# Eight filler matmuls on TensorE while VectorE finishes the last head

## The chip, the cores and the metric

One core of a Trainium2 chip. The metric is the device time of one launch in microseconds (us); lower is better. The runs of the kernel before agree within 0.2%. The profile is of one such execution, and its span, from the first to the last instruction, is some 1.9 us shorter than the device time. Every kernel here was run in the same rounds as the kernel before, on the same chip (three chips in all).

## The reference, cut to what matters

One decode step of grouped-query attention over a cache of 65,536 positions (4 key/value heads, 32 query heads of 128), mixed by a gate with a small gated MLP:

```python
def _A_ref(x, k_cache, v_cache, wq, wo):
    q = (x @ wq) ...                       # 1 x 1024 @ 1024 x 4096
    scores = einsum('bhqd,bhkd->bhqk', q, k) * Dh ** (-0.5)
    p = softmax(scores)
    o = einsum('bhqk,bhkd->bhqd', p, v)
    return o.reshape(1, 1, 4096) @ wo      # 4096 x 1024
...
return g * a + (1 - g) * b                 # g: a sigmoid gate, b: the MLP
```

There is one query row, so every weight and every cache entry is used once. The whole work is to read 162 MB and touch each number once.

## The kernel before

The end of the kernel. Per key/value head it computes scores (`k_tile`), a softmax (`stats`), and the weighted sum over V (`v_tile`). `head_out` turns one head's sum into a column block of `oa`, mostly on VectorE. `project` then multiplies `oa` by A_wo.

```python
WO_SPLIT = ((16,), (8, 4, 2, 1, 1))
...
def head_out(g):
    # DVE: mask the PSUM sum (L447), reduce it (L451)
    # PE:  L455 om_ps <- ls,hsel   (needs the softmax sums only)
    #      L457 om_ps <- o_sb,hsel (needs DVE's L451)
    # DVE: five short ops; the last (L469) writes oa
...
# the end:
for j, n, at in ((0, 2, 1), (2, 1, 3), (3, 1, 4)):
    for i, vt in enumerate(load_kv(A_v_cache, G - 1, j, at, n)):
        v_tile(G - 1, j + i, vt)
head_out(G - 1)

wo_view = A_wo.rearrange("(p c) n -> p c n", c=OC)
c0 = 0
for at, split in enumerate(WO_SPLIT):
    for n in split:
        t = load(wo_view[:, c0:c0 + n, :], (n, D), ...)
        project(t, n, oa, c0, last=(c0 + n == OC))   # 4*n matmuls of 32 columns x 256
        c0 += n
nc.scalar.copy(out=out_sb[:], in_=out_ps[:])         # then two small stores
```

The loads (`load`) are all issued by SyncE on one queue, as soon as their part of the buffer `kv` is free. PE runs its matmuls in program order.

## Time and profile before

| | before |
|---|---|
| device time, median of the first 3 runs | 383.24 us |
| span of the profile | 381.4 us |
| PE busy, DVE busy | 232.4 us (61%), 218.4 us (57%) |
| read from HBM | 162.01 MB, 425 GB/s over the span |
| mean granted TensorE clock | 0.82 |

The page of the profile cuts the span into 40 slices. A digit is the busy share in tenths (9 is 90% or more); the row PEclk is the granted TensorE clock in tenths.

```profile
PE   0433467678157944796397629872967196849355
...
PEclk9966659998759895989588959895799679969766
DMA  9999999999999999999999999999999999999995
```

The DMA engines are busy from the first slice to the last but one. No other engine is. PE (TensorE) is at nine tenths or more in 7 of the 40 slices only, and its clock keeps dropping.

The chain of waits that ended last, its end in order of time (start, length, what):

```profile
346.96 0.04 issue
347.00 31.88 DMA kv<-in_A_wo_dram
378.88 0.04 issue
378.92 0.43 PE out_ps L478 x3
379.35 0.02 issue
379.37 0.37 ACT out_sb L521
```

The chain is a load from 347.00 to 378.88. The last projection matmuls, a copy and the store follow. Only 0.43 us of this is work whose speed depends on the TensorE clock.

The timeline of PE at the end (start, length, line, what, how often; in brackets PE's idle time before it and what ended that):

```profile
359.20 5.92 PE L437 MATMUL o_ps<-kv,pt 128*64 128x512 bf16 x32 [6.08 <-DMA kv<-in_A_v_cache_dram]
365.05 0.23 PE L455 MATMUL om_ps<-ls,hsel 128*32 128x4 f32 x2
368.34 0.64 PE L457 MATMUL om_ps<-o_sb,hsel 128*32 128x128 f32 x2 [3.07 <-DVE o_sb L451]
370.37 4.62 PE L478 MATMUL out_ps<-kv,oa 128*32 128x256 bf16 x96 [1.39 <-DVE oa L469]
376.33 0.62 PE L478 MATMUL out_ps<-kv,oa 128*32 128x256 bf16 x16 [1.34 <-DMA kv<-in_A_wo_dram]
377.60 1.08 PE L478 MATMUL out_ps<-kv,oa 128*32 128x256 bf16 x12 [0.64 <-DMA kv<-in_A_wo_dram]
378.92 0.41 PE L478 MATMUL out_ps<-kv,oa 128*32 128x256 bf16 x4 [0.24 <-DMA kv<-in_A_wo_dram]
```

PE idles for 3.07 and 1.39 us while DVE works on the last head; these are the gaps that the change fills. The projection's first 96 matmuls take 4.62 us. After them PE waits for a load three more times.

In this profile the granted clock changes only at instants of a grid of 3.41 us. Busy time in stretches between such instants (stretch; its length, then PE, PEld (weight loads), DVE (VectorE), ACT, POOL busy, granted clock, DMA share, GB/s):

```profile
363.84:367.26 3.42, 1.44 (x14) 0.41 (x6) 2.07 (x2) 0.00 (x0) 0.00 (x0) 1.00 1.04 446
367.26:370.67 3.41, 0.93 (x10) 0.43 (x14) 2.23 (x6) 0.00 (x0) 0.00 (x0) 0.50 0.91 389
370.67:374.08 3.41, 3.41 (x72) 2.54 (x68) 0.00 (x0) 0.00 (x0) 0.00 (x0) 0.50 0.96 401
374.08:377.50 3.42, 1.53 (x48) 1.14 (x41) 0.00 (x0) 0.00 (x0) 0.00 (x0) 1.00 0.88 343
377.50:380.91 3.41, 1.42 (x16) 0.50 (x15) 0.00 (x0) 0.37 (x1) 0.00 (x0) 0.50 0.11 38
```

The clock is at half (0.50) in most of the projection, and again at the very end.

### The profile page before, as it was taken

Reading aid. Unit: us, or ns where it says so; the run is one execution under the profiler, and the core shown is the slowest. Engines: PE = TensorE matmul, PEld = TensorE weight load, DVE = VectorE, ACT = ScalarE, POOL = GpSimd, SP = SyncE. Lnnn points to the kernel's source line nnn. Section 1 sums busy time; section 2 is a strip of 40 time slices with the busy share of each in tenths; the row PEclk is TensorE's granted clock in tenths of the full one; section 3 lists DMA queues with packets and bytes.
Section 4 is the critical chain, followed back from the end, with each engine's and each line's share of the span. In section 5 each row is a group of like instructions: output and inputs, shape, how many; then the busy total and the mean of one; then the engine's idle time right before and its main releaser. Section 6 shows DMA issues by size and latency. Waiting matters only on the chain.

```text
span 381.4 us, 2581 instructions
## 1 busy us (share of the span) xinstructions
PE 232.4 (61%) x1372; PEld 56.8 (15%) x796; DVE 218.4 (57%) x211; ACT 39.6 (10%) x55; POOL 4.4 (1%) x10
## 2 busy tenths in 40 slices
PE   0433467678157944796397629872967196849355
PEld 0110011112011210121011101120111011212123
DVE  4241487996687506966977059669780488550040
ACT  1010001111601100114010001050001010500000
POOL 4000000000000000000000000000000000000000
PEclk9966659998759895989588959895799679969766
DMA  9999999999999999999999999999999999999995
GB/s 376 439 426 416 433 436 440 436 461 429 400 426 440 440 435 426 440 440 440 440 428 440 440 440 433 428 427 406 433 440 428 426 433 427 440 411 436 440 405 230
DMA packets 4375, 162.17 MB, mean 425 GB/s; under 512 B 520, under 2 KB 524, under 8 KB 908
## 3 DMA queue, kind: packets, MB, share of 16 engines
q1 hardware_dynamic: 4324, 162.01, 98.7%
q8 instruction: 8, 0.13, 0.1%
q14 instruction: 3, 0.02, 0.0%
q10 hardware_dynamic: 40, 0.01, 0.0%
HBM read 162.01 MB, written 0.00 MB: 425 GB/s over the span
## 4 chain that ended last, share of the span: by engine, by line
DMA 59%; PE 20%; DVE 16%; issue 2%; ACT 1%; SPq 1%; DVEq 0%; ACTq 0%
DMA kv<-in_A_k_cache_dram 37%; PE s_ps L391 15%; DVE kv L384 9%; DMA kv<-in_A_wo_dram 8%; DMA kv<-in_A_wq_dram 7%; DMA kv<-in_A_v_cache_dram 7%; PE o_ps L437 3%; DVE pt L427 2%; DVE mx L386 1%; DVE o_sb L451 1%; PE q_ps L277 1%; ACT sc L424 1%; DVE rowt L447 1%; ACT sc L402 1%; SPq L167 1%
## 5 line engine op out<-in xcount | busy, mean ns | idle before, releaser
L391 PE MATMUL s_ps<-kv,wt 128*128 128x512 bf16 x512 | 142.1, 437 | 81.8 <-DVE kv L384 81.7
L384 DVE STREAM_TRANSPOSE kv<-kv 128x2048 int32<-128x2048 int32 x64 | 142.7, 2280 | 55.5 <-DMA kv<-in_A_k_cache_dram 55.5
L437 PE MATMUL o_ps<-kv,pt 128*64 128x512 bf16 x512 | 61.6, 399 | 7.7 <-DMA kv<-in_A_v_cache_dram 7.7
L391 PEld LDWEIGHTS <-wt 128*128 128x128 bf16 x256 | 27.5, 108 | 197.6 <-issue 140.2
L402 ACT CAST sc<-s_ps 128x1024 bf16<-128x1024 f32 x16 | 16.2, 1013 | 253.5 <-PE s_ps L391 253.5
L437 PEld LDWEIGHTS <-pt 128*64 128x64 bf16 x256 | 16.0, 115 | 50.7 <-issue 48.1
L427 DVE STREAM_TRANSPOSE pt<-sc 128x1024 bf16<-128x1024 bf16 x16 | 18.6, 1217 | 6.8 <-ACT sc L424 6.8
L386 DVE TENSOR_REDUCE mx<-sc 128x1 f32<-128x1024 bf16 x12 | 14.5, 1207 | 10.1 <-ACT sc L402 10.1
L424 ACT ACTIVATE sc<-sc,nb 128x1024 bf16<-128x1024 bf16 x16 | 18.2, 1137 | 12.2 <-DVE nb L420 12.2
L447 DVE TENSOR_TENSOR rowt<-o_ps,own 128x1024 f32<-128x1024 f32 x4 | 4.8, 1194 | 24.9 <-PE o_ps L437 24.9
L457 PE MATMUL om_ps<-o_sb,hsel 128*32 128x128 f32 x8 | 2.5, 421 | 19.7 <-DVE o_sb L451 19.7
L406 DVE TENSOR_REDUCE mx<-sc 128x1 f32<-128x1024 bf16 x4 | 4.9, 1220 | 14.2 <-ACT sc L402 14.2
L277 PE MATMUL q_ps<-kv,xT 128*32 128x512 bf16 x64 | 7.2, 627 | 7.4 <-DMA kv<-in_A_wq_dram 7.4
L478 PE MATMUL out_ps<-kv,oa 128*32 128x256 bf16 x128 | 6.7, 366 | 3.7 <-DMA kv<-in_A_wo_dram 2.2
L277 PE MATMUL z_ps<-kv,xT 128*32 128x448 bf16 x64 | 6.2, 570 | 3.8 <-DMA kv<-in_B_w_in_dram 3.8
L344 DVE TENSOR_TENSOR rowt<-q_ps,own_b 128x512 f32<-128x512 f32 x2 | 1.3, 686 | 12.5 <-PE q_ps L277 12.5
L451 DVE TENSOR_REDUCE o_sb<-rowt 128x128 f32<-128x1024 f32 x4 | 7.5, 1872 | 0.1
L292 DVE TENSOR_TENSOR rowt<-z_ps,own_b 128x448 f32<-128x448 f32 x2 | 1.2, 620 | 8.5 <-PE z_ps L277 8.5
L233 PE MATMUL xb_ps<-xg,spread 8*128 8x256 bf16 x1 | 0.4, 367 | 9.1 <-DMA xg<-in_gate_w_dram 9.1
L277 PEld LDWEIGHTS <-xT 128*32 128x32 bf16 x64 | 3.0, 139 | 19.4 <-issue 19.3
L478 PEld LDWEIGHTS <-oa 128*32 128x32 bf16 x128 | 4.4, 124 | 6.1 <-issue 3.3
L521 ACT CAST out_sb<-out_ps 128x256 bf16<-128x256 f32 x1 | 0.4, 372 | 45.4 <-PE out_ps L478 45.4
(88 smaller groups left out, 54.8 us busy)
## 6 DMA issues: line engine op xcount, KB each, us to landing
kv<-in_A_k_cache_dram SPq DMA_DIRECT2D x4, 4096.0 KB, 26.8
kv<-in_A_wq_dram SPq DMA_DIRECT2D x2, 4096.0 KB, 32.8
kv<-in_A_v_cache_dram SPq DMA_DIRECT2D x2, 4096.0 KB
kv<-in_B_w_in_dram SPq DMA_DIRECT2D x2, 3584.0 KB, 15.0
kv<-in_A_wo_dram SPq DMA_DIRECT2D x1, 4096.0 KB
kv<-in_B_w_out_dram SPq DMA_DIRECT2D x1, 3584.0 KB
kv<-in_A_wo_dram SPq DMA_DIRECT2D x1, 2048.0 KB, 28.6
kv<-in_A_wo_dram SPq DMA_DIRECT2D x1, 1024.0 KB, 30.7
```

Source lines behind the costliest of these rows:

```text
L277: ins = nc.tensor.matmul(ps[t * B:(t + 1) * B, k * HN:k * HN + n], lhsT=xT[:, i * KH + c:i * KH + c + 1].to_broadcast([P, B]), rhs=w[:, c, ...
L384: nc.vector.transpose(out=kb[:, v * n:(v + 1) * n], in_=kb[:, v * n:(v + 1) * n])
L386: nc.vector.reduce_max(**late.pop())
L391: ins = nc.tensor.matmul(s_ps[:, k * HN:(k + 1) * HN], lhsT=wt[g % 2][:, v, b].rearrange("p a v h -> p (a v h)"), rhs=kx[:, b // 2, b % 2, ...
L402: nc.scalar.copy(out=sct[g, j][:], in_=s_ps[:])
L406: nc.vector.reduce_max(**late.pop())
L424: nc.scalar.activation(out=sct[g, j][:], in_=sct[g, j][:], func=ACT.Exp, scale=SCALE, bias=nb[:, 0:1], accum_out=lss[g][:, j:j + 1])
L427: nc.vector.transpose(out=ptt[g, j][:].rearrange("p c x -> p (c x)"), in_=sct[g, j][:])
L437: ins = nc.tensor.matmul(o_ps[g][hs, e, :], lhsT=ptt[g, j][:, 2 * u:2 * u + 2, :].rearrange("p c x -> p (c x)"), rhs=vx[:, 2 * u + e], sta ...
L447: nc.vector.tensor_tensor(out=om8, in0=o_ps[g][:].rearrange("p e (v d) -> p (e v) d", d=DH), in1=own_8[:].unsqueeze(2).to_broadcast([P, 2 ...
L451: nc.vector.tensor_reduce(out=o_sb[:], in_=om8.rearrange("p x d -> p d x"), axis=AX.X, op=ALU.add)
L478: nc.tensor.matmul(out_ps[t * B:(t + 1) * B, :], lhsT=vec[:, c0 + c:c0 + c + 1].to_broadcast([P, B]), rhs=w[:, c, t * NO:(t + 1) * NO], st ...
```

## The change

The intent: while VectorE finishes the last head, PE is idle, its clock is halved, and the projection runs at half speed. Eight matmuls into a spare PSUM bank, in two groups, are to keep PE busy enough that the clock stays full. Their operands are the masked weights of an earlier head (mostly zeros), and nobody reads their result.

```diff
+    def keep_busy(n):
+        ps = pss.tile([P, 2 * HN], FP32, name="busy_ps", tag="s")
+        w = wt[G % 2][:].rearrange("p v b t u h -> p (v b t u h)")
+        for i in range(n):
+            ins = nc.tensor.matmul(ps[:, :HN], lhsT=w[:, :P], rhs=w[:, :HN], start=True,
+                                   stop=True, skip_group_check=True)
+            if i > 0:
+                same_weights(ins)
...
             v_tile(G - 1, j + i, vt)
+    keep_busy(4)
     head_out(G - 1)
+    keep_busy(4)
```

In PE's program order the first group stands after the last `v_tile` and before L455; the second after L457 and before the projection. Nothing moves on the other engines. The added lines shift the later line numbers: L478 becomes L487, L521 becomes L532.

## The prediction

> **What bounds the kernel now.** Moving bytes. The profile's page shows the DMA engines at nine tenths or more in 39 of 40 slices, 162.01 MB at 425 GB/s; PE is busy 61%. The chain of waits ends in loads: A_v_cache lands at 339.7, the five A_wo loads are issued from 345.20 to 347.0, and the last one lands at 378.88. After that only this remains: the last PE matmuls of L478 (0.43 us in the chain), the ACT copy (0.37), and the store until 381.4.
>
> **What the clock does.** The windows view shows the granted clock changing between 0.50 and 1.00 only, and only on a grid of 3.413 us: up at 343.36, down at 357.02, up at 363.84, down at 367.26, up at 374.08, down at 377.50. The Trainium skill, "TensorE: Matmul & The Clock Gate", Part 1, gives a free-running window of 3413 ns: agreed. But here the clock falls without a fully idle window. PE was busy 1.44 us of 363.84-367.26, and 1.53 us of 374.08-377.50, and the clock fell; with 2.56 us of a window it stayed. Elsewhere 1.45 to 1.62 us sometimes sufficed: the boundary is near 1.5 us.
>
> **What the change adds.** Nothing is removed. Two PE groups, each one weight load and four 128x512 matmuls: one after the last v_tile, before the om_ps matmuls; one after them, before the projection. Their bank has long been free. By the trace's L437 matmuls (pairs 0.85 us apart at half clock, 0.43 at full), four cost 1.7 us cold, 0.86 warm.
> - Group 1 starts at about 365.1 with the clock full, ends about 366.0. DVE needs until 368.29 for L447 and L451, and L457 waits for that: no delay.
> - Group 2 starts about 369.0, ends at 369.8 (warm) to 370.7 (cold). The projection waits for oa, at 370.31: 0 to 0.4 us delay.
>
> **What it gains.** Group 1 lifts the window 363.84-367.26 to about 2.3 us, so the clock should no longer fall at 367.26. The next window gets L457, group 2 and the projection's start, about 1.5 us: a coin toss whether it falls at 370.67. If it stays full, the first 96 projection matmuls, 4.62 us at half clock, take an estimated 2.6 us (the 16 matmuls at 376.33, at full clock, took 0.62 with the latency of one).
>
> **How much is on the critical path.** Almost none. The 96 matmuls end at 374.99, and PE then waits 1.34 us for the next A_wo load anyway; finishing 2 us earlier only lengthens that wait. The loads were issued 18 us before the change's first instruction, so their landing doesn't move. Only the last four matmuls could gain, at most 0.2 us, if the clock were full at 378.9. But window 374.08-377.50 would hold less PE work than before, so it falls at 377.50 still.
>
> **Time.** 383.2 us, range 382.7 to 383.8; faster by over 2%: 0.01, within 2%: 0.98, slower by over 2%: 0.01.
>
> **What the profile would show.** Eight matmuls near 365 and 369; granted clock 1.00 over 367.3-370.6; the 96 matmuls shorter or the same; PE idle before 376.3 grown from 1.3 to as much as 3.3 us, ended by A_wo; last landing at 378.9 +-0.3; last four matmuls still about 0.4 us; nothing changed before 365.
>
> **What would make it wrong.** The window grid lies elsewhere in the timed runs, the last chunks at full clock (0.2 us less); a group delayed past 371.6 by an unseen semaphore; extra instruction fetches disturbing the loads; a chip with another DMA rate.

## The result

| | before | after |
|---|---|---|
| device time, median (range) of 6 runs | 383.23 us (383.12 to 383.49) | 383.29 us (383.11 to 383.39) |
| span of the profile | 381.4 us | 381.5 us |
| PE busy with the projection's matmuls on A_wo (128 of them) | 6.7 us | 5.0 us |

The ratio is 1.000 with a 95% interval of 0.9987 to 1.0013. (A ratio is the mean time of one kernel's fast runs over that of the other's in the same rounds, so it is not quite the ratio of the medians.)

The chain of waits after the change, its end:

```profile
347.20 31.77 DMA kv<-in_A_wo_dram
378.97 0.04 issue
379.01 0.43 PE out_ps L487 x4
379.44 0.02 issue
379.46 0.37 ACT out_sb L532
```

It is the same chain: the load lands at 378.97 (before: 378.88), then 0.43 us of matmuls.

The timeline of PE after the change:

```profile
365.25 1.04 PE L476 MATMUL busy_ps<-wt 128*128 128x512 bf16 x3
366.21 0.23 PE L455 MATMUL om_ps<-ls,hsel 128*32 128x4 f32 x2
368.54 0.41 PE L457 MATMUL om_ps<-o_sb,hsel 128*32 128x128 f32 x2 [2.10 <-DVE o_sb L451]
368.88 1.04 PE L476 MATMUL busy_ps<-wt 128*128 128x512 bf16 x4
370.34 1.93 PE L487 MATMUL out_ps<-kv,oa 128*32 128x256 bf16 x64 [0.43 <-DVE oa L469]
373.92 1.06 PE L487 MATMUL out_ps<-kv,oa 128*32 128x256 bf16 x32 [1.65 <-DMA kv<-in_A_wo_dram]
376.42 0.62 PE L487 MATMUL out_ps<-kv,oa 128*32 128x256 bf16 x16 [1.44 <-DMA kv<-in_A_wo_dram]
377.69 1.08 PE L487 MATMUL out_ps<-kv,oa 128*32 128x256 bf16 x12 [0.64 <-DMA kv<-in_A_wo_dram]
379.01 0.40 PE L487 MATMUL out_ps<-kv,oa 128*32 128x256 bf16 x4 [0.24 <-DMA kv<-in_A_wo_dram]
```

(One of the first group's four records is missing from the trace.) The groups do what they were made for. The first 96 matmuls of the projection take 1.93 + 1.06 = 2.99 us instead of 4.62. But the row that was one is now two: after 64 matmuls PE waits 1.65 us for the next chunk of A_wo, which lands at about 373.9. Before, the first 64 matmuls at half clock were done at about that time (68 had started by 373.90), so no wait showed. The 1.6 us saved is now waiting, and the chunk after that starts at 376.42, as before (376.33).

The same stretches after the change, on this execution's grid:

```profile
364.15:367.57 3.42, 2.23 (x16) 0.39 (x6) 2.19 (x2) 0.00 (x0) 0.00 (x0) 1.00 0.97 417
367.57:370.98 3.41, 2.02 (x30) 0.86 (x31) 2.11 (x6) 0.00 (x0) 0.00 (x0) 1.00 0.97 413
370.98:374.39 3.41, 1.76 (x68) 1.54 (x64) 0.00 (x0) 0.00 (x0) 0.00 (x0) 1.00 0.97 400
374.39:377.80 3.41, 1.33 (x45) 0.93 (x37) 0.00 (x0) 0.00 (x0) 0.00 (x0) 1.00 0.83 324
377.80:381.21 3.41, 1.25 (x16) 0.34 (x9) 0.00 (x0) 0.37 (x1) 0.00 (x0) 0.50 0.07 26
```

The clock stays full over two boundaries where it was halved before, and then falls at 377.80, because the stretch before that held only 1.33 us of PE work. The last matmuls, the only ones on the chain, run at half clock exactly as before.

### The profile page after: what moved, and what is told of

Same layout as the page of the kernel before. It is cut to its first block, busy times and chain, and to the rows that moved or that the text cites. A ratio compares the mean times of both kernels' runs of the same rounds, so it can differ in the third digit from the quotient of the medians.

```text
span 381.5 us, 2590 instructions
## 1 busy us (share of the span) xinstructions
PE 232.8 (61%) x1379; PEld 56.1 (15%) x798; DVE 218.5 (57%) x211; ACT 39.6 (10%) x55; POOL 4.4 (1%) x10
## 4 chain that ended last, share of the span: by engine, by line
DMA 58%; PE 25%; DVE 13%; ACT 2%; issue 1%; SPq 0%; DVEq 0%; ACTq 0%
DMA kv<-in_A_k_cache_dram 41%; PE s_ps L391 21%; DMA kv<-in_A_wo_dram 8%; DVE kv L384 7%; DMA kv<-in_A_v_cache_dram 7%; PE o_ps L437 3%; DVE pt L427 2%; DMA xg<-in_A_x_dram 2%; DVE o_sb L451 1%; DVE mx L386 1%; ACT sc L402 1%; ACT sc L424 1%; DVE rowt L447 1%; SPq L167 0%; PE om_ps L457 0%
## 5 line engine op out<-in xcount | busy, mean ns | idle before, releaser
L437 PE MATMUL o_ps<-kv,pt 128*64 128x512 bf16 x512 | 61.8, 400 | 7.5 <-DMA kv<-in_A_v_cache_dram 7.5
L437 PEld LDWEIGHTS <-pt 128*64 128x64 bf16 x256 | 16.1, 115 | 50.6 <-issue 48.1
L457 PE MATMUL om_ps<-o_sb,hsel 128*32 128x128 f32 x8 | 2.3, 386 | 18.7 <-DVE o_sb L451 18.7
L487 PE MATMUL out_ps<-kv,oa 128*32 128x256 bf16 x128 | 5.0, 286 | 4.5 <-DMA kv<-in_A_wo_dram 4.0
L532 ACT CAST out_sb<-out_ps 128x256 bf16<-128x256 f32 x1 | 0.4, 372 | 45.2 <-PE out_ps L487 45.2
L487 PEld LDWEIGHTS <-oa 128*32 128x32 bf16 x128 | 3.4, 97 | 6.7 <-issue 5.3
```

Of the source, the lines that this page charges most:

```text
L437: ins = nc.tensor.matmul(o_ps[g][hs, e, :], lhsT=ptt[g, j][:, 2 * u:2 * u + 2, :].rearrange("p c x -> p (c x)"), rhs=vx[:, 2 * u + e], sta ...
L487: nc.tensor.matmul(out_ps[t * B:(t + 1) * B, :], lhsT=vec[:, c0 + c:c0 + c + 1].to_broadcast([P, B]), rhs=w[:, c, t * NO:(t + 1) * NO], st ...
```

## The experiments

Three theories:

- **A.** The landing of the last A_wo load sets the end; PE's speed before it is slack, and the clock can only matter for the last chunk's matmuls.
- **B.** The gain is real but was lost because the clock fell at 377.80, before the last chunks.
- **C.** The groups cost what the clock gains.

Nine kernels were run, one of them (e2) twice. All results were correct except where a wrong one was intended.

### e1: the clock full to the very end

```diff
             project(t, n, oa, c0, last=(c0 + n == OC))
+            keep_busy({16: 4, 8: 4, 4: 2}.get(n, 0))
```

> The changed kernel plus groups of 4, 4 and 2 more busy matmuls after the projections of the first three A_wo chunks, so that the clock stays full until the last matmul. Theory A (the landing of the last A_wo load sets the end): the clock reads 1.00 to the end, the last chunk's four matmuls take about 0.27 us instead of 0.40, the last landing stays at 378.9 +-0.2, time 383.1, at most 0.2 us below the kernel before. Theory B (the gain was lost because the clock fell at 377.80, before the last chunks): 1 us or more faster, 382.2 or less. Theory C (the groups cost what the clock gains): slower than the changed kernel, by up to the 2.2 us that ten more matmuls take at full clock.

Measured: median 383.23 us (383.01 to 383.34), ratio 1.0001 (0.9988 to 1.0014). The last two rows of its PE timeline, where the granted clock reads 1.00:

```profile
378.12 0.29 PE L487 MATMUL out_ps<-kv,oa 128*32 128x256 bf16 x4 [0.27 <-DMA kv<-in_A_wo_dram]
378.77 0.29 PE L487 MATMUL out_ps<-kv,oa 128*32 128x256 bf16 x4 [0.36 <-DMA kv<-in_A_wo_dram]
```

The last four matmuls take 0.29 us instead of 0.40 to 0.41. So the whole possible gain of a full clock at the end is 0.12 us, 0.03% of the time, which the runs can't resolve. Theory B falls. Theory C's loss isn't there either.

### e2 and e3: no A_wo loads, without and with the groups

Both leave out all the loads of A_wo, six in number: the first half in one piece, issued at 333 us in the kernel before, and the five of the second half, which alone the prediction and the expectations count. They project whatever lies in the buffer. The result is wrong (relative error 0.03). e2 is the kernel before with this edit, e3 the changed kernel with it.

```diff
-        t = load(wo_view[:, c0:c0 + n, :], (n, D), at + ...)
+        o0 = int((at + ...) * CT * P)
+        t = kv[:, o0:o0 + n * D].rearrange("p (a b) -> p a b", b=D)
```

> The kernel before with the five A_wo loads left out; the projection reads whatever lies in the buffer, so the result is wrong on purpose. Theory A: the last DMA wait is then A_v_cache's at 359.2, oa comes at 370.3 as before, the 128 projection matmuls run without a stop, at half clock until about 374.1 and then full, some 5.2 us, so the time falls by 3 to 4.5 us, to about 379 to 380. If the loads did not set the end, the time would fall by less than 1 us.

> The changed kernel (both groups) with the five A_wo loads left out; wrong result on purpose. Theory A: without the loads the projection is on the chain, at full clock, about 3.6 us for 128 matmuls, so this kernel is 1.3 to 2 us faster than the same kernel without the groups (the run sent with it). Theory C: no faster than that, since what the clock gains is eaten by the groups themselves.

> The same kernel as e2_noload_plain again, because the profiled execution of that run fell in a state in which every matmul took about twice as long as at half clock (span 794 us) and shows nothing of the tail. Theory A: a fast profile shows the 128 projection matmuls start at about 370.4 without a stop after oa, in 4.5 to 5.5 us against 3.68 in e3_noload_groups, with the clock at half for most of them; time 378.3 to 381.2 as in the fast runs of the first try.

| | fast runs | median | ratio to the kernel before (95%) |
|---|---|---|---|
| e2, without groups | 5 | 380.00 us (378.31 to 381.17) | 0.9908 (0.9889 to 0.9927) |
| e3, with groups, same rounds as e2 | 4 | 377.97 us (377.73 to 378.37) | 0.9864 (0.9851 to 0.9876) |
| e2b, e2 again, later | 4 | 378.64 us (378.39 to 379.71) | 0.9883 (0.9868 to 0.9898) |

The profiled execution of e2 is left out: it fell in a slow state (796.12 us) that is told in the last section. The projection in e2b, then in e3, from their timelines of PE:

```profile
370.30 5.46 PE L487 MATMUL out_ps<-kv,oa 128*32 128x256 bf16 x128 [1.39 <-DVE oa L469]
```

```profile
370.66 3.68 PE L487 MATMUL out_ps<-kv,oa 128*32 128x256 bf16 x128 [0.43 <-DVE oa L469]
```

With the loads gone, the projection runs without a stop and stands on the chain. Now the groups make the projection 1.78 us shorter in the traces (5.46 - 3.68; it ends only 1.43 us earlier, at 374.37 against 375.80, since `oa` came 0.36 us later in e3's execution), and the runs of the same rounds differ by 1.7 us in the mean (379.71 and 378.01). This is what the change was meant to gain, and it is a real gain where nothing hides it. Theory C falls: the groups themselves cost nothing there. With the loads in place the same speed-up moved nothing. e2b's runs came out nearer to e3 than e2's did (0.8 us from e3's mean, in other rounds, and the two intervals overlap a little; e2b's profiled execution was the slowest of its four). So the gain is some 0.8 to 1.7 us. That its size depends on how the clock's grid fell is likely, but not shown.

The times fell by 3.5 to 5.2 us (differences of the means from the kernel before of the same rounds), which the loads had added to the end.

### e4 and e5: delay the projection

The second group is made longer, 44 or 16 matmuls instead of 4.

```diff
     head_out(G - 1)
-    keep_busy(4)
+    keep_busy(44)    # e4;  16 in e5
```

> The changed kernel with 44 instead of 4 matmuls in the second group: 9.5 us at full clock, so the projection starts near 378.5 instead of 370.34. Theory A: the slack before the loads, an estimated 5 us (all 128 matmuls back to back take about 3.6 us and must end at 379.4), swallows most of the 8.1 us of delay; 2.4 to 3.2 us slower, 385.7 to 386.5. If PE's work set the end (against A): slower by the whole 8.1 us, 391.

> The changed kernel with 16 instead of 4 matmuls in the second group, so that the projection starts about 2.1 us later, near 372.4. Theory A: the slack swallows all of it: 383.2 +-0.2, the last four matmuls at 378.8 to 379.0. Theory C or any theory in which PE's work before the last load counts: 385.3.

e4: 386.17 us (385.29 to 387.46), ratio 1.0078 (1.0066 to 1.0091). The end of its chain:

```profile
368.79 9.39 PE busy_ps L476 x43
378.18 0.15 issue
378.32 3.71 PE out_ps L487 x128
382.03 0.02 issue
382.05 0.37 ACT out_sb L532
```

The projection starts 7.98 us later than in the changed kernel (378.32 against 370.34), but the means differ from the kernel before by only 3.0 us (386.23 against 383.22). Five microseconds of delay vanish. Now PE is on the chain, and the load is not.

e5: 383.10 us (383.03 to 383.27), ratio 0.9995 (0.9979 to 1.0012). The first and the last row of the projection in its timeline of PE:

```profile
372.33 2.80 PE L487 MATMUL out_ps<-kv,oa 128*32 128x256 bf16 x96
378.83 0.29 PE L487 MATMUL out_ps<-kv,oa 128*32 128x256 bf16 x4 [0.36 <-DMA kv<-in_A_wo_dram]
```

The projection starts at 372.33, 2 us later, and nothing is lost. The last four matmuls start at 378.83. A change that makes PE's work there 2 us later costs as little as one that makes it 1.6 us shorter gains. Both are theory A.

### e6 and e7: one group alone

```diff
-    keep_busy(4)     # left out in e7
     head_out(G - 1)
-    keep_busy(4)     # left out in e6
```

> Only the first group. Clock: stays full over the window boundary near 367.3 to 367.6 and falls one window later, near 371, so that most of the first 96 projection matmuls run at half clock, ending near 374.7. Time by theory A the same, 383.2 +-0.2.

> Only the second group. Clock: falls near 367.3 to 367.6 as in the kernel before, the group runs at half clock (1.7 us, to about 370.8, so the projection starts some 0.4 us later than before), the window to 371 holds about 2.6 us of PE work, which is at or under what raised the clock in the kernel before (2.57 did not, 2.84 did), so it rises only near 374.4 or with luck at 371. Time by theory A the same, 383.2 +-0.2; if PE's delay counted, 0.4 us slower.

Times: e6 383.26 us (383.21 to 383.29), ratio 0.9998 (0.9983 to 1.0013); e7 383.09 us (383.05 to 383.21), ratio 0.9994 (0.9979 to 1.0009). Neither moved, as expected.

The clock: in e7 it fell at 367.17 and rose at 373.99, as in the kernel before; the second group alone comes too late, and with 2.00 us of PE work in the stretch from 367.17 it doesn't bring the clock back. Its last matmuls ran at full clock all the same (0.29 us), since its stretch from 373.99 held 1.67 us of work and the clock stayed. e6 doesn't test the first group cleanly. Its grid lay about 1.4 us earlier relative to its work (boundaries at 362.40, 365.81, 369.23), the clock fell at 369.23 after a stretch with 0.41 us of PE work, and most of the first 64 projection matmuls ran at half clock (3.45 us). The expectation had it fall near 371. Its granted clock also reads 0.95 where the other profiles read 1.00, from 55.2 us on. What the first group alone does on the usual grid stays open; for the time it doesn't matter.

### e8 and e9: is there a faster version?

Seen in the kernel before, the DMA share falls from 1.0 at 376.25 us to 0.6 at 377 and to nothing at 378.5. Perhaps the small last chunks of A_wo waste DMA time, and a full clock would allow larger ones.

```diff
-WO_SPLIT = ((16,), (8, 4, 2, 1, 1))
+WO_SPLIT = ((16,), (8, 4, 4))       # e9: (8, 6, 2)
...
+            if c0 + n < OC:
+                keep_busy({16: 4, 8: 4, 4: 3}.get(n, 0))   # e9: {16: 4, 8: 4, 6: 2}
```

> Is there a faster version? The second half of A_wo in chunks of 8, 4, 4 instead of 8, 4, 2, 1, 1, with busy groups of 4, 4 and 3 after the first three chunks so that the clock is full at the end. In the kernel before, the DMA engines' share falls from 1.0 at 376.25 to 0.6 at 377 and to 0 at 378.5, and the last load lands at 378.88. If the small chunks cost DMA time, the last load lands 0.3 to 0.8 us earlier; the 16 matmuls behind it take about 0.62 us at full clock instead of 0.41 at half: 382.6 to 383.1. If the engines' different ends are not due to the chunks' size, the landing stays within 0.2 us and the time is 383.4.

> The same with chunks of 8, 6, 2 and busy groups of 4, 4 and 2: the last chunk has 8 matmuls, about 0.40 us at full clock, as much as four took at half clock. If the small chunks cost DMA time, landing 0.2 to 0.5 us earlier and 382.8 to 383.1; if not, 383.2 to 383.3.

e8: 383.37 us (383.17 to 383.48), ratio 1.0004 (0.9991 to 1.0016). From the chain of e8:

```profile
346.52 32.30 DMA kv<-in_A_wo_dram
378.81 0.04 issue
378.86 0.64 PE out_ps L487 x16
```

The last load lands at 378.81 with three chunks in the second half as with five (378.88), so the chunks' size is not what thins out the DMA at the end; the hoped-for gain was a miss. All that changed is 0.2 us more of matmuls behind it. e9: 383.19 us (383.10 to 383.23), ratio 0.9999 (0.9986 to 1.0013): no different. In its profile the last filler group was still running at 378.85 and stood on the chain for 0.54 us. The profile's list of DMA issues has the last load landing 33.2 us after its issue at 345.47, so at about 378.7; with five chunks it landed between 378.73 (e1) and 378.97 (the changed kernel), so this is no clear gain either.

e9 shows something more. Up to the projection it is the changed kernel, with both groups, but its grid lay some 1.4 us earlier than in the changed kernel's profile. The stretch from 366.14 to 369.56 held only L457 and the second group, 1.37 us of PE work, and the clock fell. The first 64 matmuls then took 3.57 us, mostly at half clock, instead of 1.93:

```profile
369.56 3.57 PE L487 MATMUL out_ps<-kv,oa 128*32 128x256 bf16 x64 [0.43 <-DVE oa L469]
```

So the two groups don't hold the clock on every position of the grid. Of the seven profiles of kernels with both groups, six kept it full up to the projection (the changed kernel, e1, e3, e8, and e4 and e5 with a longer second group). e9's time was no different for it.

Why the DMA engines finish at different times is left open. No version beat the kernel before.

## Why the prediction was right

- **What bounds the kernel.** Held. The chain ends in the A_wo load in both kernels, and taking the loads away shortened the run by 3.5 to 5.2 us (e2, e2b, e3).
- **The clock.** Held, with luck at one point. The first group kept the clock full at the boundary 367.57. The next boundary was called a coin toss; the stretch held 2.02 us, more than the 1.5 us expected, and the clock stayed. That the grid lay well for the groups was luck too: in e9 it lay elsewhere and the clock fell before the projection. The call that it would fall again before the last chunks was right (377.80), for the reason given: faster matmuls leave less busy time in the last stretch.
- **The cost of the groups.** Held. Group 1 was through when L455 started at 366.21, L457 came 0.2 us later with everything else of this execution, and `oa` was not delayed.
- **The gain off the chain.** The estimate of 2.6 us for 96 matmuls was somewhat low: 2.99 us in two pieces here, 2.80 us in one piece in e5.
- **The shape of the wait.** The prediction put all of the new idle time ahead of 376.3, "as much as 3.3 us". In the run it is split: 1.65 us ahead of 373.92 and 1.44 us ahead of 376.42, 3.09 us together. I had overlooked that the second chunk's load lands only near 373.9, which before was covered by PE's own slowness. The sum was right, the place was not.
- **The critical path.** At most 0.2 us was allowed for the last four matmuls. e1 measured 0.12 us when the clock is full there; in the changed kernel itself it is nothing.
- **The time.** 383.2 us predicted, 383.29 us measured. The change did its stated job, a full clock through most of the projection, and the time didn't move, because the speed-up became a wait for a load that had been issued 18 us earlier. That the DMA engines set when it lands is read from the profile, where they are busy to the last slice but one; no run here changed their rate.

## What to carry to other kernels

Before you repair a slow engine, follow the chain of waits from the end and ask what the engine waits for next: if that is a load already on its way, the repair only lengthens the wait. To know what a repair would be worth, remove the thing that hides it (here the loads: 0.8 to 1.7 us appeared), and to know how much slack there is, delay the same work on purpose (here 5 of 8 us vanished). Filler matmuls held the clock in six of seven profiles, so they are worth trying where PE comes last and no load does; but look at more than one execution, since where the clock's grid lies decides whether a given group is enough.

## What the Trainium skill lacked or had wrong

- "TensorE: Matmul & The Clock Gate", Part 1, gives a free-running window of 3413 ns; agreed: the boundaries in the traces lie 3.41 us apart, from the first change to the last. Its table, though, lets the clock fall after one or more idle windows, and the rule under "Why this matters for your kernels" is to avoid idle gaps over some 3 us. (A later paragraph of Part 1 does tell of a kernel whose short idles between groups of matmuls let the clock swing, without a figure for how much idle is too much.) Here it fell after windows that were far from idle: 1.44 us and 1.53 us of PE work of 3.41 (kernel before), 1.33 us (changed kernel). It fell after 1.37 us in e9, too. With 1.66 us (e5), 1.67 us (e7) and 1.76 us (changed kernel) it stayed. The kernel before also has windows with 1.45 and 1.62 us in which it stayed, so the boundary lies about 1.5 us by this profile's busy time and is not sharp in it. This holds only after a profile's first change of the clock: until then the row reads 1.00 even where PE does nothing (from 2.03 to 8.85 us in the kernel before). In the kernel before the clock fell at 367.26, 2.0 us after PE's last matmul.
- The same page says nothing about filler work of zeros. The groups, whose operands are mostly zeros, kept the clock full over 367.57 and 370.98 in the changed kernel (in e9 they didn't suffice). No run here tried operands other than these. The page's remark on zeros concerns another limiter.
- The page warns that the clock has been seen stuck at a quarter for over 50 us. In one execution, the profiled one of e2, something like it lasted all the launch: 796.12 us instead of 380, with 32 of the L437 matmuls in 13.16 us, where at half clock they need an estimated 6.8 us (from the 0.85 us between weight-load pairs in the kernel before, eight of which make up the 32). The profile's clock row was empty there (it reads 1.00), so a quarter clock is inferred from the durations, not shown. It was the only such execution of e2, whose other five runs took 378 to 381 us.
- No page has a granted clock of 0.95. In e6's profile the clock alternates between 0.50 and 0.95, and the weight-load pairs of L437 lie 0.45 us apart at 0.95, where they lie 0.43 us apart at 1.00 in the kernel before. No run here shows why.
- No page gives a figure for what the grid's position costs at the end of a kernel, where PE is on the chain (what the same page says of the window's phase concerns the start). e2's five fast runs spread over 2.9 us (378.31 to 381.17), the kernel before in the same rounds over 0.4 us (382.99 to 383.37), and e3, with the groups, over 0.6 us. That the grid is the cause is argued, not shown: only one execution of a kernel has a trace, and the others don't tell where it lay.
